# Three loads moved behind the first exchange of values and the transposes of a fused attention and feed-forward kernel

## The chip, the cores and the metric

The kernel runs on one core of a Trainium2 chip. The metric is the device time of one execution in microseconds (us). Three executions of the kernel before took 244.43, 244.81 and 245.82 us; their median is 244.81 us. The profile is of a further execution of its own.

## The reference, cut to what matters

The input x has 2048 rows of 512 bf16 numbers. It is normalised row by row, and the result feeds two branches. The output is x plus both.

```python
xn = _layernorm(x, axis=-1)
return x + _A_ref(xn, A_wq, A_wk, A_wv, A_wo, A_beta) + _B_ref(xn, B_w1, B_w2)

# A: 32 heads of 16 numbers, 4 segments of 512 rows, one after the other
logits = jnp.einsum('bhqd,bhkd->bhqk', qs, ks) * scale + mask    # causal, inside a segment
a_dot = jnp.einsum('bhqk,bhkd->bhqd', _softmax(logits, axis=-1), vs)
a_mem = num / den                        # phi(qs) against M and z of the segments before
o = g * a_mem + (1.0 - g) * a_dot        # g = sigmoid(beta), one number a head
M = M + jnp.einsum('bhld,bhle->bhde', phi(ks), vs)
z = z + jnp.einsum('bhld->bhd', phi(ks))
# then  o @ wo

# B: a feed-forward layer with 1792 hidden columns
out = jnp.einsum('bsf,fd->bsd', _silu(jnp.einsum('bsd,df->bsf', x, w1)), w2)
```

## The kernel before, in words

The work goes by the four segments of 512 rows (`NSEG`), and inside a segment by four slices of 128 columns (`DT`), each of which holds 8 heads. A slice of a segment is called u (u = 4 s + dt).

Per segment the rows are normalised (`ln`, lines 542 to 608): VectorE takes statistics of a block of 128 rows (BN_STATS, BN_AGGR), GpSimd makes the inverse deviation, VectorE writes the normalised block xn, and xn is transposed into xnT. For the first segment TensorE transposes; for the others SP issues a DMA transpose (line 602). xn lies in a ring of three buffers, so the fourth xn of a segment can't be written before the first transpose of it has landed. From xnT come k and q by slice (`k_tile`, `q_tile`), the values V (`v_tile`) and the hidden tiles h (`h_tile`: four matmuls into a PSUM bank, a tanh on ScalarE at line 1093, a multiply on VectorE at line 1097 which reads that bank for the last time).

The scores are worked in quads (`quad`, line 795): one quad fills four PSUM banks (psS), ScalarE takes the exponential of all of it (line 818), GpSimd cuts out what the causal mask forbids (line 834). There are 72 quads, nine for two slices. `pv` (line 848) multiplies the five quads of a slice by the values; it accumulates into two of four PSUM banks (ps), one for even and one for odd heads. Half of its matmuls read V, the other half VS, a copy of V with the upper and lower 64 partitions exchanged. `v_swap` (line 762) makes that copy with two DMAs of SP: the exchange of values. VectorE evicts the two banks to N and O (line 877).

phi(k) is made by ScalarE, GpSimd and VectorE in pkT, a ring of two, and transposed by DMA into phiK (line 709), from which the memory M is summed at the segment's end. den and norm work out the two divisors: VectorE and GpSimd make a small table, which goes out to DRAM and is read back in another shape (dD to Dg, dE to Dr, dZ to Zg, dR to R), all of it issued by SP; VectorE and GpSimd then multiply by it. `w2_rows` and `wo_rows` make the output rows of a segment during the next one.

What stands in which order on each engine isn't written out by hand. `Sched` (lines 98 to 261) plays the whole program through once with estimated durations while the kernel is built: each task has an engine, a duration, a time `vis` after which its result is taken to be there, a due time and the tasks it waits for; the ready task with the lowest due time goes next. The instructions are then emitted in that order, and each engine, SP among them, runs them strictly in order. `Dn(n)` is the due time of quad n: 12.5 + 2.3 n. A due time or a `vis` changes the order, not what is waited for on the chip.

All loads from DRAM stand at the beginning (lines 399 to 424). SP issues in this order: two blocks of x, half of wk, wv, half of w1, half of wk, the second 512 rows of x in two loads, the second half of w1, beta, wo, all of w2 (1792 KB), rows 1024 to 1535 of x (x8, the third block). ScalarE's queue issues two blocks of x and wq. The load of the last 512 rows (x12) waits for a free place in `x_all`, which holds three blocks. Only after these does SP come to the exchange of values and to the DMA transposes of the second segment.

Of the kernel before, what the change touches and what calls it, by code (L numbers as in the profile page):

```python
# [23 lines left out]
TPS = L // P  # L24
F = 1792
FT = F // P
# [238 lines left out]
def kernel(  # L265
# [38 lines left out]
    x_b = [Buf(x_r) for _ in range(NSEG)]  # L304
# [7 lines left out]
    w_o = sb([P, DT, D], BF16, "w_o")  # L312
# [58 lines left out]
    def Dn(n):  # L371
        return T0 + CYC * n
# [2 lines left out]

    xl = {}

    def load_x(t, n, eng, due, vis):
        def fn():
            e = nc.sync if eng == "SP" else nc.scalar  # L380
            c = x_b[t // TPS].idx * TPS + t % TPS
            e.dma_start(
                out=x_all[:, c : c + n, :],
                in_=x_flat[t * P : (t + n) * P, :].rearrange("(j p) d -> p j d", p=P),
            )
        k = A(eng, 0.5, fn, due=due, vis=vis, takes=(x_b[t // TPS],), label=f"x{t}")
        for i in range(n):
            xl[t + i] = k

    def load_w(dst, src, eng, due, vis):  # L390
        def fn():
            e = nc.sync if eng == "SP" else nc.scalar
            e.dma_start(out=dst, in_=src)
        return A(eng, 0.5, fn, due=due, vis=vis, label="w")

    def kv(w):
        return w.rearrange("(ko ki) n -> ki ko n", ki=P)
# [5 lines left out]
    def halves(dst, src, n, which):  # L403
        c = slice(0, n) if which == 0 else slice(n, None)
        return dst[:, :, c], kv(src)[:, :, c]

    C2, F2 = D // 2, F // 2
    ld_k = [load_w(*halves(w_k, A_wk, C2, 0), "SP", 0, 5.2)]
    ld_q = [load_w(*halves(w_q, A_wq, C2, 0), "ACTQ", 0, 5.4)]
    ld_v = load_w(w_v[:], kv(A_wv), "SP", 0, 7.5)  # L410
# [7 lines left out]
        bet[:], bass.AP(tensor=A_beta.tensor, offset=A_beta.offset, ap=[[0, P], [1, H]]),  # L418
        "SP", 0.35, 13.5,
    )  # L420
    ld_o = load_w(w_o[:], kv(A_wo), "SP", 0.4, 14.0)
    ld_2 = load_w(w_2[:], kv(B_w2), "SP", 0.5, 18.0)
    load_x(8, 4, "SP", 0.6, 19.0)
    load_x(12, 4, "SP", 0.7, 8.0)

    def pool(dur, fn, deps=(), due=0.0, **k):
        return A("POOL", dur, fn, deps, due, **k)

# [333 lines left out]
    def v_swap(s, due):  # L762
        ts = []
        for r in range(2):
            def f(r=r):
                a, b = slice(KB * r, KB * r + KB), slice(KB * (1 - r), KB * (1 - r) + KB)
                nc.sync.dma_start(out=VS_t[a, :, :], in_=V_t[V_b[s].idx][b, :, :])
            ts.append(A("SP", 0.6, f, v_ev[s], due, vis=6.0 if s == 0 else 4.2, takes=(VS_b[s],),
                        frees=(V_b[s], VS_b[s]), label="VS"))
        vs_ev[s] = ts  # L770

# [332 lines left out]
    def w2_rows(s, j, due):  # L1104
        t = s * TPS + j
        b = Buf(banks)
        ab = Buf(acc_r)

        def s2(ft):
            def f():  # L1110
                mm(b.tile[:], h_b[(s, ft)].tile[:, j * P : (j + 1) * P], w_2[:, ft, :],
                   ft == 0, ft == FT - 1)
            return (f, 0.216, (h_ev[(s, ft)],) + ((ld_2,) if ft == 0 else ()))

        g = group(b, [s2(ft) for ft in range(FT)], due, keep=1,
                  deps=[h_ev[(s, ft)] for ft in range(FT)], label=f"w2.{t}")
        for ft in range(FT):
            h_b[(s, ft)].n += 1
            g.frees.append(h_b[(s, ft)])

        def f_e():
            nc.vector.scalar_tensor_tensor(
                out=ab.tile[:], in0=b.tile[:], scalar=0.5, in1=xt(t), op0=ALU.mult,
                op1=ALU.add,
            )
        e = A("DVE", 0.6, f_e, [g], due + 4, takes=(ab,), frees=(b, ab, x_b[s]), label="acc")
        acc_ev[t] = (ab, e)

    def wo_rows(s, j, due):
        t = s * TPS + j  # L1130
        b = Buf(banks)
        ab, ae = acc_ev[t]

        def so(dt):
            def f():
                mm(b.tile[:], N_b[s].tile[:, dt, j * P : (j + 1) * P], w_o[:, dt, :],
                   dt == 0, dt == DT - 1)
            return (f, 0.216, (oT_ev[4 * s + dt],) + ((ld_o,) if dt == 0 else ()))

        g = group(b, [so(dt) for dt in range(DT)], due, keep=1,  # L1140
                  deps=[oT_ev[4 * s + dt] for dt in range(DT)], label=f"wo.{t}")
        N_b[s].n += 1
        g.frees.append(N_b[s])
        ob = Buf(o_r)

        def f_e():
            nc.vector.scalar_tensor_tensor(
                out=ob.tile[:], in0=b.tile[:], scalar=0.5, in1=ab.tile[:], op0=ALU.mult, op1=ALU.add
            )
        e = A("DVE", 0.6, f_e, [g, ae], due + 2, takes=(ob,), frees=(b, ab, ob), label="o_t")  # L1150

        def f_d():
            nc.sync.dma_start(out=out_flat[t * P : (t + 1) * P, :], in_=ob.tile[:])
        A("SP", 0.35, f_d, [e], due + 4, vis=1.75, frees=(ob,), label="out")

    def tail():
# [34 lines left out]
        for j in range(TPS):  # L1191
# [13 lines left out]
                nc.sync.dma_start(out=out_flat[t * P : (t + 1) * P, :], in_=ob.tile[:])  # L1205
            A("SP", 0.35, f_d, [e], 0, vis=1.75, frees=(ob,), label="out")

    ln(0, -4)
    for s in range(NSEG):
        b0 = 20 * s  # L1210
        if s + 1 < NSEG:
            ln(s + 1, Dn(1) if s == 0 else Dn(b0 - 4))
        if s == 0:
            for dt in range(DT):
                k_tile(0, dt, -2.9 if dt == 0 else Dn(5 * dt - 3 - dt % 2))
                q_tile(0, dt, -3 if dt == 0 else Dn(5 * dt - 2.9 - dt % 2))
# [67 lines left out]
```

## Time and profile before

| | us |
|---|---|
| Median of three executions | 244.81 |
| The profiled execution, its own time | 243.62 |
| Its span, first to last instruction | 241.9 |

So 1.7 us of the profiled execution lie around its span. In the span TensorE (PE) is busy 223.8 us, ScalarE (ACT) 178.5, VectorE (DVE) 170.2 and GpSimd (POOL) 164.0. The mean granted clock of TensorE is 0.979 of full speed.

The timeline has a row for each instruction or run of like instructions: its start, its length, engine, line, operation, output from input, count, and in brackets the idle time of its engine just before it with what ended that. SPq is SP's queue, where a row's length is the time that issuing took and not the time of the transfer; PEld is the loading of weights. The table of windows has, for each stretch, its length, the busy time and the count of instructions of PE, PEld, DVE, ACT and POOL, the granted clock, the mean busy share of the 16 DMA engines and the GB/s that they moved.

### The profile page before, as it was taken

The numbers are of one execution on the slowest core, as the hardware profiler recorded it, in microseconds if no ns is written. First come the engines' busy times: TensorE is split into PE (matmuls) and PEld (weight loads), VectorE is DVE, ScalarE is ACT, GpSimd is POOL, SyncE is SP. The second block draws the span as 40 slices with busy tenths as digits, with TensorE's granted clock in tenths as the row PEclk, the third lists the DMA queues.
The fourth block names the chain that finished last, engine by engine and source line by source line (L and its number), as shares of the span: only waits on it lengthen the run. The fifth ranks groups of instructions, "written<-read, shape, count | busy, mean of one in ns | idle before, by whom it ended". The sixth has DMA issues, their size and how long they took to land.

```text
span 241.9 us, 6809 instructions
## 1 busy us (share of the span) xinstructions
PE 223.8 (93%) x2812; PEld 104.8 (43%) x2812; DVE 170.2 (70%) x299; ACT 178.5 (74%) x160; POOL 164.0 (68%) x279
## 2 busy tenths in 40 slices
PE   7899579998999997999799999999998999999974
PEld 7644144433444433444344434454435433444431
DVE  4699497957977536799884599775656685576523
ACT  2599837997999793898797997788899888862000
POOL 7359838996997617799887789897755667454010
PEclk9999968999999997999999999999999999999999
DMA  6999940200354324311153320102352000143202
GB/s 191 354 357 335 143 63 3 45 2 3 65 103 100 91 79 125 101 45 30 39 119 73 85 54 3 43 8 98 101 121 72 27 4 11 25 121 107 69 25 87
DMA packets 31068, 21.33 MB, mean 88 GB/s; under 512 B 16116, under 2 KB 30140, under 8 KB 31036
## 3 DMA queue, kind: packets, MB, share of 16 engines
q1 hardware_dynamic: 29692, 20.10, 32.0%
q10 hardware_dynamic: 1344, 0.79, 1.1%
q8 instruction: 22, 0.36, 0.7%
q14 instruction: 10, 0.08, 0.1%
HBM read 11.87 MB, written 2.65 MB: 60 GB/s over the span
## 4 chain that ended last, share of the span: by engine, by line
PE 39%; POOL 16%; DMA 15%; DVE 12%; ACT 10%; SPq 4%; issue 3%; POOLq 0%; ACTq 0%; DVEq 0%
PE ps L500 32%; ACT Pt L818 8%; POOL Pt L834 8%; PE psS L500 6%; DMA xnT<-xn 3%; POOL kB L695 3%; DMA R<-dR 2%; DVE st L550 2%; SPq L1031 2%; DMA Dg<-dD 2%; POOL pq L999 2%; ACT hT L1093 2%; DMA dR<-Zr 2%; DVE hT L1097 2%; DMA Dr<-dE 1%
## 5 line engine op out<-in xcount | busy, mean ns | idle before, releaser
L818 ACT ACTIVATE Pt<-psS 128x2048 bf16<-128x2048 f32 x72 | 135.3, 1879 | 31.2 <-PE psS L500 26.5
L834 POOL TENSOR_SCALAR_AFFINE_SELECT Pt<-Pt 64x512 bf16<-64x512 bf16 (+1 forms) x144 | 95.2, 661 | 36.1 <-ACT Pt L818 30.9
L500 PE MATMUL ps<-xnT,w 128*128 128x512 bf16 x224 | 57.0, 383 | 0.1
L500 PE MATMUL ps<-w,hT 128*128 128x512 bf16 x196 | 48.7, 380 | 0.0
L1097 DVE SCALAR_TENSOR_TENSOR hT<-hT,ps 128x512 bf16<-128x512 bf16 x56 | 37.3, 679 | 10.6 <-ACT hT L1093 10.5
L1093 ACT ACTIVATE hT<-ps 128x512 bf16<-128x512 f32 x56 | 32.5, 599 | 4.9 <-PE ps L500 4.8
L500 PE MATMUL psS<-qT,kB 32*128 32x256 bf16 (+5 forms) x640 | 29.3, 267 | 2.6 <-ACT Pt L818 2.5
L500 PEld LDWEIGHTS <-w 128*128 128x128 bf16 x224 | 20.5, 99 | 25.7 <-issue 4.1
L500 PEld LDWEIGHTS <-hT 128*128 128x128 bf16 x224 | 20.3, 98 | 24.6 <-issue 3.1
L500 PE MATMUL ps<-Pt,VS 64*32 64x256 bf16 (+5 forms) x640 | 20.1, 273 | 4.7 <-DVE hT L1097 4.5
L500 PEld LDWEIGHTS <-kB 32*128 32x128 bf16 x640 | 12.4, 93 | 27.4 <-issue 25.1
L695 POOL TENSOR_SCALAR kB<-kT,pm 128x512 bf16<-128x512 bf16 x30 | 20.8, 702 | 4.2 <-DVE kT L690 2.7
L500 PE MATMUL ps<-Pt,V 64*32 64x256 bf16 (+5 forms) x640 | 21.8, 271 | 0.0
L500 PE MATMUL ps<-xnT,w_k 128*128 128x512 bf16 (+1 forms) x76 | 19.7, 366 | 0.5 <-DVE N L877 0.5
L877 DVE CAST N<-ps 128x512 bf16<-128x512 f32 x16 | 11.0, 687 | 12.0 <-PE ps L500 11.9
L500 PE MATMUL ps<-xnT,w_q 128*128 128x512 bf16 (+1 forms) x76 | 17.3, 346 | 2.2 <-DVE hT L1097 1.2
L999 POOL TENSOR_TENSOR pq<-pq,Dr 128x512 bf16<-128x512 bf16 x12 | 13.8, 1158 | 6.2 <-DMA Dr<-dE 5.9
L500 PEld LDWEIGHTS <-V 64*32 64x32 bf16 x640 | 14.1, 94 | 8.5 <-DVE hT L1097 2.5
L500 PE MATMUL ps<-w_o,N 128*128 128x512 bf16 x56 | 15.1, 384 | 1.2 <-DVE hT L1097 1.2
L500 PE MATMUL ps<-w_v,xnT 128*128 128x512 bf16 x64 | 16.0, 380 | 0.0
L500 PEld LDWEIGHTS <-VS 64*32 64x32 bf16 x640 | 13.0, 94 | 6.4 <-issue 3.8
L1063 DVE TENSOR_TENSOR N<-N,R 128x512 bf16<-128x512 bf16 x16 | 7.9, 500 | 9.6 <-DMA R<-dR 9.6
(82 smaller groups left out, 247.6 us busy)
## 6 DMA issues: line engine op xcount, KB each, us to landing
VS<-V SPq DMA_DIRECT2D x8, 264.0 KB
R<-dR SPq DMA_DIRECT2D x16, 128.0 KB
out_dram<-o_t SPq DMA_DIRECT2D x16, 128.0 KB
w<-in_B_w_dram SPq DMA_DIRECT2D x2, 896.0 KB
w<-in_B_w_dram SPq DMA_DIRECT2D x1, 1792.0 KB
Dr<-dE SPq DMA_DIRECT2D x12, 128.0 KB
x_all<-in_A_x_dram SPq DMA_DIRECT2D x2, 512.0 KB
N<-O SPq DMA_DIRECT2D x12, 64.0 KB
```

The lines of the kernel that those rows point to most:

```text
L500: nc.tensor.matmul(o, lhsT=l, rhs=r, start=start, stop=stop, **k)
L550: nc.vector.bn_stats(out=b.tile[:], in_=xt(t))
L695: nc.gpsimd.tensor_scalar(out=kB[u].tile[:, :, KB * r : KB * r + KB], in0=kT[u].tile[:].rearrange("p (a b) -> p a b", b=KB), scalar1=pm[:, ...
L818: nc.scalar.activation(out=pb.tile[:], in_=psS[:], func=AF.Exp, scale=SCALE)
L834: nc.gpsimd.affine_select(out=v, in_=v, compare_op=ALU.is_ge, fill=0.0, base=0, pattern=pat, channel_multiplier=-1,)
L877: nc.vector.tensor_copy(out=dst.tile[:, dt, :], in_=buf.tile[:])
L999: nc.gpsimd.tensor_tensor(out=pb.tile[:], in0=pb.tile[:], in1=rb.tile[:], op=ALU.mult)
L1031: nc.sync.dma_start(out=N_b[s].tile[r, ds, :], in_=O_b[s].tile[r, ds, :])
L1063: nc.vector.tensor_tensor(out=v, in0=v, in1=rb.tile[:], op=ALU.mult)
L1093: nc.scalar.activation(out=hb.tile[:], in_=b.tile[:], func=AF.Tanh, scale=0.5)
L1097: nc.vector.scalar_tensor_tensor(out=hb.tile[:], in0=hb.tile[:], scalar=1.0, in1=b.tile[:], op0=ALU.add, op1=ALU.mult)
```

## The change

Four loads leave the head of SP's list: wo, w2, x8 and x12. w2 is cut into two halves of 896 KB. A new function `late_loads`, called after the normalisation of the second segment has been entered, gives them due times and a time before which the planner doesn't place them. A row of `w2_rows` waits for the second half of w2 only from its eighth matmul on. The planner's `vis` of the first exchange of values goes from 6.0 to 4.2, that of all others. No arithmetic changes.

```diff
-    ld_o = load_w(w_o[:], kv(A_wo), "SP", 0.4, 14.0)
-    ld_2 = load_w(w_2[:], kv(B_w2), "SP", 0.5, 18.0)
-    load_x(8, 4, "SP", 0.6, 19.0)
-    load_x(12, 4, "SP", 0.7, 8.0)
...
-            ts.append(A("SP", 0.6, f, v_ev[s], due, vis=6.0 if s == 0 else 4.2, takes=(VS_b[s],),
+            ts.append(A("SP", 0.6, f, v_ev[s], due, vis=4.2, takes=(VS_b[s],),
...
-            return (f, 0.216, (h_ev[(s, ft)],) + ((ld_2,) if ft == 0 else ()))
+            return (f, 0.216, (h_ev[(s, ft)], ld_2[ft >= FT // 2]))
...
+    def late_loads():
+        def at(k, n):
+            k.ready = Dn(n)
+            return k
+
+        c = slice(0, FT // 2), slice(FT // 2, FT)
+        for i, n in ((0, 6), (1, 9)):
+            ld_2.append(at(load_w(w_2[:, c[i], :], kv(B_w2)[:, c[i], :], "SP", Dn(n), 5.5), n))
+        ld_o.append(at(load_w(w_o[:], kv(A_wo), "SP", Dn(12), 4.5), 12))
+        load_x(8, 4, "SP", Dn(14), 4.5)
+        load_x(12, 4, "SP", Dn(15), 8.0, [xl[8]])
+        at(xl[8], 14)
...
             ln(s + 1, Dn(1) if s == 0 else Dn(b0 - 4))
+            if s == 0:
+                late_loads()
```

The planner makes a new order of it on every engine. Three places matter. The first is SP's list after beta. Before, wo, w2 and x8 stand ahead of the exchange (VS) and of the transposes of the second segment (xnT1).

```order
L393 DMA bet_182<-in_A_beta_dram 128x32
L393 DMA w_o_74<-in_A_wo_dram 128x4x512
L393 DMA w_2_76<-in_B_w2_dram 128x14x512
L382 DMA x_all_70<-in_A_x_dram 128x4x512
L767 DMA VS_97<-V0_95 64x2112 x2
L602 DMA_TRANSPOSE xnT1_78<-xn1_80 128x4x128
L602 DMA_TRANSPOSE xnT1_78<-xn2_81 128x4x128
L602 DMA_TRANSPOSE xnT1_78<-xn0_79 128x4x128
L602 DMA_TRANSPOSE xnT1_78<-xn1_80 128x4x128
```

In the changed kernel the same place reads:

```order
L393 DMA bet_182<-in_A_beta_dram 128x32
L763 DMA VS_97<-V0_95 64x2112 x2
L598 DMA_TRANSPOSE xnT1_78<-xn1_80 128x4x128
L598 DMA_TRANSPOSE xnT1_78<-xn2_81 128x4x128
L598 DMA_TRANSPOSE xnT1_78<-xn0_79 128x4x128
L598 DMA_TRANSPOSE xnT1_78<-xn1_80 128x4x128
L393 DMA w_2_76<-in_B_w2_dram 128x7x512
L705 DMA_TRANSPOSE phiK0_100<-pkT0_98 128x4x128
L705 DMA_TRANSPOSE phiK0_100<-pkT1_99 128x4x128
L393 DMA w_2_76<-in_B_w2_dram 128x7x512
L393 DMA w_o_74<-in_A_wo_dram 128x4x512
L705 DMA_TRANSPOSE phiK0_100<-pkT0_98 128x4x128
```

The exchange and the four transposes now stand ahead of all late loads; the first half of w2 stands between the transposes of xn and those of phi(k), the rest follows after two of these. The load of x8 stands behind the last row shown, and the fourth transpose of phi(k) behind that.

The second place is on VectorE, from the last normalised block of the second segment (written into xn1) to the eviction of the first `pv` to N0. Before:

```order
L568 TENSOR_SCALAR xn1_80<-x_all_70,mv_153,rstd_154 128x512
L485 TENSOR_REDUCE gsum_184<-gm_183 128x3
L632 SCALAR_TENSOR_TENSOR pkT0_98,zc0_166<-kT0_82,pkT0_98 128x512
L550 BN_STATS st0_155<-x_all_70 128x6
L551 BN_AGGR mv_153<-st0_155 128x2
L1097 SCALAR_TENSOR_TENSOR hT3_117<-hT3_117,ps3_69 128x512
L632 SCALAR_TENSOR_TENSOR pkT1_99,zc0_166<-kT1_83,pkT1_99 128x512
L550 BN_STATS st1_156<-x_all_70 128x6
L551 BN_AGGR mv_153<-st1_156 128x2
L550 BN_STATS st2_157<-x_all_70 128x6
L551 BN_AGGR mv_153<-st2_157 128x2
L877 CAST N0_136<-ps0_66 128x512
```

In the changed kernel:

```order
L564 TENSOR_SCALAR xn1_80<-x_all_70,mv_153,rstd_154 128x512
L481 TENSOR_REDUCE gsum_184<-gm_183 128x3
L628 SCALAR_TENSOR_TENSOR pkT0_98,zc0_166<-kT0_82,pkT0_98 128x512
L1093 SCALAR_TENSOR_TENSOR hT3_117<-hT3_117,ps3_69 128x512
L628 SCALAR_TENSOR_TENSOR pkT1_99,zc0_166<-kT1_83,pkT1_99 128x512
L873 CAST N0_136<-ps0_66 128x512
```

The statistics of the third block (its x8 isn't there yet) have left this place; the four of them now stand some thirty rows further on, 14 instructions behind the third phi(k). hT3 is the last reader of bank ps3, which the first `pv` takes next. On TensorE nothing moves up to and with that first `pv` and the quad behind it.

The third place is on SP in the second segment, where the divisors are read back. Before:

```order
L963 DMA dD1_198<-den0_152 4x8x512
L709 DMA_TRANSPOSE phiK0_100<-pkT0_98 128x4x128
L1048 DMA dR0_192<-Zr0_176 128x128
L709 DMA_TRANSPOSE phiK0_100<-pkT1_99 128x4x128
L1055 DMA R0_139<-dR0_192 128x1x512
L1055 DMA R1_140<-dR0_192 128x1x512
L1055 DMA R2_141<-dR0_192 128x1x512
L969 DMA Dg1_179<-dD1_198 128x128
```

In the changed kernel:

```order
L959 DMA dD1_198<-den0_152 4x8x512
L1044 DMA dR0_192<-Zr0_176 128x128
L965 DMA Dg1_179<-dD1_198 128x128
L705 DMA_TRANSPOSE phiK0_100<-pkT0_98 128x4x128
L1051 DMA R0_139<-dR0_192 128x1x512
L1051 DMA R1_140<-dR0_192 128x1x512
L1051 DMA R2_141<-dR0_192 128x1x512
```

The read of Dg now stands ahead of the three reads of R and of both transposes. On VectorE the reciprocal of Dg moves ahead of the first multiply by R, where it stood behind it. Everything behind the first `pv` is ordered anew in this way, on all engines.

More of the change, by code (lines that the diff above doesn't have):

```diff
@@ L376, with load_x @@
     xl = {}
-    def load_x(t, n, eng, due, vis):
+    def load_x(t, n, eng, due, vis, after=()):
         def fn():
@@ L385, in fn, with load_w @@
             )
-        k = A(eng, 0.5, fn, due=due, vis=vis, takes=(x_b[t // TPS],), label=f"x{t}")
+        k = A(eng, 0.5, fn, due=due, vis=vis, seqdeps=after, takes=(x_b[t // TPS],), label=f"x{t}")
         for i in range(n):
             xl[t + i] = k
-    def load_w(dst, src, eng, due, vis):
+    def load_w(dst, src, eng, due, vis, after=()):
         def fn():
@@ L393, in fn @@
             e.dma_start(out=dst, in_=src)
-        return A(eng, 0.5, fn, due=due, vis=vis, label="w")
+        return A(eng, 0.5, fn, due=due, vis=vis, seqdeps=after, label="w")
     def kv(w):
@@ L407 @@
     C2, F2 = D // 2, F // 2
+    ld_o, ld_2 = [], []
     ld_k = [load_w(*halves(w_k, A_wk, C2, 0), "SP", 0, 5.2)]
@@ L1137, in f @@
                    dt == 0, dt == DT - 1)
-            return (f, 0.216, (oT_ev[4 * s + dt],) + ((ld_o,) if dt == 0 else ()))
+            return (f, 0.216, (oT_ev[4 * s + dt], ld_o[0]))
         g = group(b, [so(dt) for dt in range(DT)], due, keep=1,
```

## The prediction

> **What bounds the kernel now.** The page of the profile comes first: its span, TensorE's share, the granted clock and the traffic in 40 slices of 6.05 us each.
>
> ```profile
> span 241.9 us, 6809 instructions
> PE 223.8 (93%) x2812; PEld 104.8 (43%) x2812; DVE 170.2 (70%) x299; ACT 178.5 (74%) x160; POOL 164.0 (68%) x279
> PE   7899579998999997999799999999998999999974
> PEclk9999968999999997999999999999999999999999
> GB/s 191 354 357 335 143 63 3 45 2 3 65 103 100 91 79 125 101 45 30 39 119 73 85 54 3 43 8 98 101 121 72 27 4 11 25 121 107 69 25 87
> ```
>
> TensorE is the bound: 93% of the span. It falls off at two places before the tail, and at both the clock falls too: slices 5 and 6 (24 to 36 us) and the neighbourhood of slice 16 (91 to 97 us). The first lies where DMA traffic of 335 to 357 GB/s ends. So I read that place next, in the timeline of each engine, TensorE first.
>
> ```profile
> 27.06 0.40 PE L500 MATMUL ps<-Pt,V 64*32 64x512 bf16 x4
> 31.10 0.40 PE L500 MATMUL ps<-Pt,VS 64*32 64x512 bf16 x8 [3.64 <-DVE hT L1097]
> 27.90 0.09 PEld L500 LDWEIGHTS <-VS 64*32 64x32 bf16 x1 [0.74 <-DMA VS<-V]
> 33.52 1.88 ACT L818 ACTIVATE Pt<-psS 128x2048 bf16<-128x2048 f32 x1 [3.39 <-PE psS L500]
> ```
>
> The first `pv` begins at 27.06 and stands still for 3.64 us before its second bank. VS was late, but it was there at 27.90; what ends the wait is VectorE's hT, the last reader of that bank. ScalarE's exponentials wait 3.39 us in turn. Why hT came so late stands in VectorE's timeline and in the chain of waits, SP's issues beside them.
>
> ```profile
> 24.45 0.54 DVE L568 TENSOR_SCALAR xn<-x_all,mv,rstd 128x512 bf16<-128x512 bf16 x1
> 28.47 0.41 DVE L568 TENSOR_SCALAR xn<-x_all,mv,rstd 128x512 bf16<-128x512 bf16 x1 [3.48 <-DMA xnT<-xn]
> 30.39 0.66 DVE L1097 SCALAR_TENSOR_TENSOR hT<-hT,ps 128x512 bf16<-128x512 bf16 x1
> 20.13 8.25 DMA xnT<-xn
> 10.58 1.20 SPq L393 DMA_DIRECT2D w<-in_B_w_dram  x1
> 11.82 5.84 SPq L382 DMA_DIRECT2D x_all<-in_A_x_dram  x1
> 17.79 1.98 SPq L767 DMA_DIRECT2D VS<-V  x2
> ```
>
> VectorE needs the xn buffer that the first transpose reads. That transpose was issued at 20.13 and took 8.25 us to land, since wo, w2 and x8 were queued ahead. The same backlog blocked SP for 5.84 us in issuing x8. VectorE runs in order, so hT waited behind xn, and TensorE behind hT.
>
> **What the stall costs.** These are windows of the same trace.
>
> ```profile
> 18.00:24.00 6.00, 6.00 (x45) 2.52 (x44) 5.96 (x12) 5.80 (x6) 5.71 (x10) 1.00 1.12 340
> 31.10:39.00 7.90, 7.38 (x112) 3.54 (x112) 7.14 (x19) 4.50 (x4) 3.70 (x7) 0.57 0.17 36
> 31.50:32.00 0.50, 0.50 (x41) 0.50 (x28) 0.50 (x3) 0.00 (x0) 0.00 (x0) 0.53 1.15 250
> 38.00:38.50 0.50, 0.50 (x3) 0.18 (x2) 0.47 (x2) 0.50 (x1) 0.25 (x1) 0.65 0.00 0
> 24.00:60.00 36.00, 30.34 (x419) 13.56 (x418) 27.43 (x56) 27.84 (x28) 26.98 (x45) 0.91 0.31 44
> ```
>
> Behind the stall the clock is at half from about 31.5 to 38.2 us. From 31.10 to 39.00 TensorE was busy 7.38 us at a mean clock of 0.57, so 7.38 x 0.43 = 3.2 us of its work was lost beside the wait. The Trainium skill ("TensorE: Matmul & The Clock Gate", section on the HAM clock gate) says that an idle window of about 3.4 us halves the clock and a busy one of 3.4 us restores it; by one such window the loss would be an estimated 1.7 us and the sum 1.5 us smaller. The trace shows 6.7 us of half clock here, and I keep 3.2.
>
> **The change, part by part.**
>
> *The queue.* The loads kept ahead are eight blocks of x (1024 KB), wk, wq and wv (1536) and w1 (1792): 4352 KB, or 4.46 MB. Slices 1 and 2 of the page move 6.05 x (191 + 354) = 3.30 MB by 12.1 us; the other 1.16 MB at 357 GB/s are through by 15.3. The loads taken out are 2816 KB or 2.88 MB, 8.5 us at the 340 GB/s of the window of 18 to 24.
>
> ```profile
> 15.38 0.69 DVE L755 CAST V<-ps 128x512 bf16<-128x512 f32 x1
> 129.40 1.85 DMA Zg<-dZ
> 136.30 3.27 DMA R<-dR
> L709 SPq DMA_TRANSPOSE phiK<-pkT x12: 1190/1214/2017, 30.2 to 151.6; - x12
> 26.58 0.59 ACT L1093 ACTIVATE hT<-ps 128x512 bf16<-128x512 f32 x1
> 28.80 0.24 DVE L485 TENSOR_REDUCE gsum<-gm 128x3 f32<-128x96 f32 x1
> 28.96 0.68 DVE L632 SCALAR_TENSOR_TENSOR pkT<-kT,pkT 128x512 bf16<-128x512 bf16 x1
> 29.57 0.69 DVE L550 BATCH_NORM_STATS2 st<-x_all 128x6 f32<-128x512 bf16 x1
> 30.29 0.18 DVE L551 BATCH_NORM_AGGREGATE mv<-st 128x2 f32<-128x6 f32 x1
> ```
>
> V is complete at 16.07, so VS is issued into an empty queue. Two issues took 1.98 us; with 3.27 us to land, as a read of R in mid-kernel, VS is there by 21.3, nearly 6 us before it is wanted. The first xn is no earlier than before (its x is not among the moved loads), so its transpose is issued at 20.13 again. It takes 1.2 us to issue (the row of phiK: median 1214 ns). If its landing is like that of R, it is there by 24.6; the fourth xn wants the buffer at 24.99, the end of the third. VectorE's 3.48 us are gone, by a margin of 0.4.
>
> *The first `pv`.* hT needs the tanh, which ends at 27.17, as before: ScalarE ran ahead of the stall. VectorE gets there by 24.99 + 0.41 + 0.24 + 0.68 = 26.3 (xn, the sum for the gate, phi(k)), since the pair of statistics has gone. hT ends at 27.17 + 0.66 = 27.83, and TensorE goes on at 27.9 in place of 31.10: **3.2 us**. A wait of 0.45 us is left. I take the half clock to go with the long wait: **3.2 us** more.
>
> *The late loads.* SP ends its fourth transpose of xn near 27.4 (two issues of 1.2 from 24.99), issues half of w2, then the transposes of phi(k). Half of w2 is 0.92 MB, 2.7 us at 340 GB/s; the transpose behind it can land anywhere from 31 (nothing queued: 27.9 + 1.2 + 1.85, the landing of the small read of Zg) to 35 (the whole load, then 3.27). The reader of its buffer is ScalarE, whose next exp into pkT follows one quad:
>
> ```profile
> 28.95 1.08 ACT L1093 ACTIVATE hT<-ps 128x512 bf16<-128x512 f32 x2
> 35.29 0.62 ACT L623 ACTIVATE pkT<-kT 128x512 bf16<-128x512 bf16 x1
> 36.87 1.88 ACT L818 ACTIVATE Pt<-psS 128x2048 bf16<-128x2048 f32 x1 [0.96 <-POOL Pt L834]
> ```
>
> ScalarE ends its two tanh at 30.0, takes the quad (1.88) and the gate's tanh and wants pkT at about 32.1. The next exponential is queued behind that. So this costs 0 to 2.9 us; I take **-0.6**, since a quad of its own work lies in front. The second half of w2 and wo follow 2 us later; w2 is first read in the second segment, and nobody waits for it.
>
> *The statistics of the third block.* Four pairs of some 0.8 us (0.69 and 0.18, a little overlapped), three of which lay in the stall at no cost, now stand in a full stretch: 3.3 us of VectorE, 0 to 3.3 on the path. From 24 to 60 VectorE is busy 27.43 of 36 us; with 6.4 us less of span 2.2 us stay free. I take **-0.5**.
>
> *The second place.* SP's new order there touches a stall of the same build.
>
> ```profile
> 84.50 0.39 SPq L969 DMA_DIRECT2D Dg<-dD  x1
> 85.27 0.43 DVE L1063 TENSOR_TENSOR N<-N,R 128x512 bf16<-128x512 bf16 x1 [1.16 <-DMA R<-dR]
> 89.25 0.95 DVE L973 RECIPROCAL Dg<-Dg 128x128 f32<-128x128 f32 x1 [3.55 <-DMA Dg<-dD]
> 91.48 0.81 PE L500 MATMUL ps<-w_o,N 128*128 128x512 bf16 x3 [1.19 <-DVE hT L1097]
> 93.25 0.61 PE L500 MATMUL ps<-Pt,VS 64*32 64x512 bf16 x8 [0.63 <-DVE hT L1097]
> 90.00:98.00 8.00, 6.19 (x102) 2.86 (x100) 5.78 (x12) 4.06 (x3) 5.23 (x8) 0.79 0.40 120
> 82.45 1.94 SPq L1055 DMA_DIRECT2D R<-dR  x3
> ```
>
> Dg is issued at 84.50, behind a transpose (1.2) and three reads of R (1.94). VectorE waits for it 3.55 us, TensorE for VectorE 1.19 + 0.63 = 1.8 us, and the clock costs 6.19 x 0.21 = 1.3. With Dg ahead of these reads it comes some 3 us sooner. So up to 3.1 us are to be had; as the new order is new everywhere behind 30 us, the same may be lost elsewhere. Bounds 3.1 either way; I take **+1.0**, a third, because only this one place can be read from the order.
>
> Sum: 3.2 + 3.2 - 0.6 - 0.5 + 1.0 = **6.3 us**. From the profiled execution's 243.62 that is 237.3. The median of the runs is 1.19 us above that execution; from 244.81 it is **238.5 us**.
>
> **The rivals.**
>
> *Given back by engines that are full.* From 24 to 60 the four engines were busy 27 to 28 us each (TensorE 30.34 with 3.2 lost to the clock). In 29.6 us all would stand at 91 to 94%. In-order engines that full wait for each other. If a further 3 to 5 us of the 6.3 are given back, the time is 241.5 to 243.6. For it: ScalarE and VectorE were busy nearly as long as TensorE there. Against it: work can slip to 60 to 90 us, and TensorE at 93% of a span shows that it can be kept fed.
>
> *The change doesn't do what it says.* VS and xnT are late anyway, because the queue is still full or the transposes are slow, and hT waits as before: within 1.2 us of 244.8. For it: the margin of 0.4 us at xn, and a transpose in an empty queue isn't in the trace. Against it: the 8.5 us of transfers that stood in front are more than the 3.5 us of wait.
>
> *Slower: x8 comes too late.* x8 is now issued behind the third transpose of phi(k). VectorE reads it 14 instructions after writing that phi(k), at some 0.6 us each 8.4 us later; the transpose's issue, its own (a third of 1.94), 0.52 MB at 340 GB/s and the landing take 1.2 + 0.65 + 1.5 + 3.3 = 6.7. If it lands later, VectorE stands at the statistics, and queued behind them are the evictions of the third `pv`, so TensorE's banks stay full: the stall of before at another place, priced at its wait plus 3.2 us of clock. To lose more than the 6.3 + 1.2 us it has to wait over 4.3 us, which is to land over 6.0 us later than worked out here. Then the time is over 246. For it: x8 blocked SP for 5.84 us before, and w2's half and wo (1.4 MB, 4.2 us) go just ahead. Against it: they go out near 32 and should be through by 38, before x8 is issued. The Trainium skill ("DMA: Bandwidth & Descriptors", rules for kernel authors) says to issue a DMA early and wait late; by that rule the change has nothing to win. Here the early issue is what held the short transfers up.
>
> **How the numbers follow.** A measurement of this kernel can tell about 0.5%, 1.2 us, from no change. The forecast (faster by 3.3 us or more, likeliest 238.5) gets 0.66, gains given back to 241.5 to 243.6 gets 0.16, no effect 0.09, slower 0.09. So faster is 0.82, the same 0.09, slower 0.09. The best ends give 3.2 + 3.2 + 3.1 = 9.5 us or 235.3, with 0.4 us of spread between runs 234.9. Leaving out no effect and slower leaves out 0.18; the range is 234.9 to 243.4.
>
> **What would show it.** Right: no wait of VectorE for xnT near 25 us; the first matmul with VS by 28; a granted clock of 1.00 from 28 to 40; the eighth exponential near 30 in place of 33.52; at the second place, VectorE's wait for Dg under 2 us. Wrong: ScalarE idle before pkT near 32, VectorE idle before a BN_STATS near 50, or a new slice with half the clock behind a wait of over a microsecond.

## The result, and the profile after

The changed kernel takes 237.96 us (median of four executions, 236.88 to 238.85). The kernel before took 244.62 us beside it (243.88 to 245.82). The ratio is 0.9721, with a 95% interval of 0.966 to 0.9783: faster by 2.8%. The forecast was 238.5 us. Here and below the ratios leave out executions over 1.5% above the fastest of their kernel, the medians count all.

The profiled execution of the changed kernel took 238.85 us with a span of 237.1. First its page: span, busy shares, granted clock and traffic in 40 slices, here of 5.93 us each.

```profile
span 237.1 us, 6771 instructions
PE 218.1 (92%) x2780; PEld 105.0 (44%) x2812; DVE 171.1 (72%) x299; ACT 178.4 (75%) x160; POOL 163.2 (69%) x279
PEclk9999999999999999999999999999999999999999
GB/s 196 352 218 125 54 290 151 113 22 4 93 140 69 108 178 88 48 3 68 94 91 62 90 25 0 46 28 113 61 110 17 83 1 19 39 91 136 58 22 88
```

No slice of PEclk is below 9: both dips of the clock are gone. The traffic that stood in slices 3 to 5 has moved to slices 6 to 8 (30 to 47 us). Next the timeline where the stall was: TensorE, VectorE, ScalarE and SP's issues, in this order.

```profile
27.33 0.40 PE L496 MATMUL ps<-Pt,V 64*32 64x512 bf16 x4
28.21 0.40 PE L496 MATMUL ps<-Pt,VS 64*32 64x512 bf16 x8 [0.48 <-DVE hT L1093]
24.70 1.18 DVE L564 TENSOR_SCALAR xn<-x_all,mv,rstd 128x512 bf16<-128x512 bf16 x2
27.47 0.69 DVE L1093 SCALAR_TENSOR_TENSOR hT<-hT,ps 128x512 bf16<-128x512 bf16 x1 [0.46 <-ACT hT L1089]
30.18 1.90 ACT L814 ACTIVATE Pt<-psS 128x2048 bf16<-128x2048 f32 x1
34.20 0.63 ACT L619 ACTIVATE pkT<-kT 128x512 bf16<-128x512 bf16 x1 [2.04 <-DMA phiK<-pkT]
34.73 1.86 ACT L814 ACTIVATE Pt<-psS 128x2048 bf16<-128x2048 f32 x1
20.38 7.38 SPq L598 DMA_TRANSPOSE xnT<-xn  x4
27.81 0.58 SPq L393 DMA_DIRECT2D w<-in_B_w_dram  x1
28.48 2.52 SPq L705 DMA_TRANSPOSE phiK<-pkT  x2
31.06 0.57 SPq L393 DMA_DIRECT2D w<-in_B_w_dram  x1
```

The last two blocks of xn now run back to back (24.70, x2): VectorE no longer waits for xnT. hT waits only for its tanh, TensorE 0.48 us instead of 3.64, and the eighth exponential starts at 30.18 instead of 33.52. But a new wait stands behind it: ScalarE waits 2.04 us for a transpose of phi(k), issued at 28.48 behind half of w2. In the windows of this trace (length, busy time of PE, PEld, DVE, ACT, POOL, then the clock, DMA share and GB/s) it shows as idle TensorE.

```profile
28.00:40.00 12.00, 9.51 (x151) 4.66 (x159) 7.21 (x17) 9.78 (x11) 8.34 (x15) 1.00 0.81 228
34.00:38.00 4.00, 2.31 (x14) 0.92 (x13) 0.69 (x1) 3.71 (x4) 2.23 (x4) 1.00 1.10 340
```

From 34 to 38 us TensorE is busy only 2.31 of 4 us, while 340 GB/s of late loads arrive; its clock stays at 1.00.

The nth of the 72 exponentials is a clock that all versions share, since its order never changes. Its start in the two profiled executions, from ScalarE's rows:

| exponential | before | after | ahead by |
|---|---|---|---|
| 7 (the first behind the stall) | 33.52 | 30.18 | 3.34 |
| 8 | 36.87 | 34.73 | 2.14 |
| 10 | 43.57 | 39.62 | 3.95 |
| 14 | 54.09 | 50.76 | 3.33 |
| 15 | 58.33 | 53.27 | 5.06 |
| 27 | 89.81 | 85.10 | 4.71 |
| 28 (the second place) | 95.95 | 88.33 | 7.62 |
| 36 | 119.15 | 109.80 | 9.35 |
| 37 | 121.92 | 114.58 | 7.34 |
| 71 (the last) | 213.03 | 207.05 | 5.98 |
| end of span | 241.9 | 237.1 | 4.8 |

The number counts from 0. The gain comes up to 7, from 8 to 10, from 14 to 15, from 27 to 28 and up to 36; part of it goes again at 8, from 10 to 14, at 37 and behind. Two executions can't tell what of this is the change and what is chance: the medians differ by 6.66 us, these two by 4.77. That is what the experiments are for.

### The profile page after: what moved, and what is told of

It is laid out like the page before. It is cut to its first block, busy times and chain, and to the rows that moved or that the text cites. A ratio compares the mean times of both kernels' runs of the same rounds, so it can differ in the third digit from the quotient of the medians.

```text
span 237.1 us, 6771 instructions
## 1 busy us (share of the span) xinstructions
PE 218.1 (92%) x2780; PEld 105.0 (44%) x2812; DVE 171.1 (72%) x299; ACT 178.4 (75%) x160; POOL 163.2 (69%) x279
## 4 chain that ended last, share of the span: by engine, by line
PE 57%; POOL 12%; DMA 9%; ACT 9%; DVE 6%; issue 4%; SPq 2%; ACTq 0%; POOLq 0%; DVEq 0%
PE ps L496 47%; PE psS L496 10%; ACT Pt L814 7%; POOL Pt L830 6%; DMA phiK<-pkT 4%; DMA R<-dR 3%; POOL kB L691 2%; ACT hT L1089 2%; DMA dR<-Zr 2%; DVE hT L1093 1%; DVE pkT L628 1%; SPq L1051 1%; POOL pkT L622 1%; POOL pq L622 1%; DVE pq L628 1%
## 5 line engine op out<-in xcount | busy, mean ns | idle before, releaser
L830 POOL TENSOR_SCALAR_AFFINE_SELECT Pt<-Pt 64x512 bf16<-64x512 bf16 (+1 forms) x144 | 93.1, 647 | 40.5 <-ACT Pt L814 34.4
L496 PE MATMUL ps<-w,hT 128*128 128x512 bf16 x184 | 45.9, 380 | 1.2 <-issue 1.1
L496 PE MATMUL psS<-qT,kB 32*128 32x256 bf16 (+5 forms) x640 | 28.7, 261 | 4.9 <-ACT Pt L814 4.3
L496 PEld LDWEIGHTS <-w 128*128 128x128 bf16 x224 | 19.7, 97 | 24.8 <-issue 3.7
L691 POOL TENSOR_SCALAR kB<-kT,pm 128x512 bf16<-128x512 bf16 x30 | 22.2, 748 | 4.4 <-DVE kT L686 3.1
L496 PE MATMUL ps<-Pt,V 64*32 64x256 bf16 (+5 forms) x640 | 20.7, 260 | 0.0
L496 PE MATMUL ps<-Pt,VS 64*32 64x256 bf16 (+5 forms) x640 | 18.7, 261 | 1.2 <-DVE hT L1093 1.2
L496 PE MATMUL ps<-xnT,w_k 128*128 128x512 bf16 (+1 forms) x73 | 17.3, 344 | 0.9 <-DVE N L873 0.5
L496 PE MATMUL ps<-w_o,N 128*128 128x512 bf16 x54 | 14.1, 380 | 0.2 <-issue 0.2
L628 DVE SCALAR_TENSOR_TENSOR pkT<-kT,pkT 128x512 bf16<-128x512 bf16 x12 | 10.7, 889 | 4.7 <-POOL pkT L622 4.7
```

The costliest lines, as they stand in the source:

```text
L496: nc.tensor.matmul(o, lhsT=l, rhs=r, start=start, stop=stop, **k)
L628: nc.vector.scalar_tensor_tensor(out=dst_b.tile[:], in0=src_b.tile[:], scalar=0.0, in1=dst_b.tile[:], op0=ALU.max, op1=ALU.add, accum_out=acc,
L691: nc.gpsimd.tensor_scalar(out=kB[u].tile[:, :, KB * r : KB * r + KB], in0=kT[u].tile[:].rearrange("p (a b) -> p a b", b=KB), scalar1=pm[:, ...
L830: nc.gpsimd.affine_select(out=v, in_=v, compare_op=ALU.is_ge, fill=0.0, base=0, pattern=pat, channel_multiplier=-1,)
```

## The experiments

Most edits stand at the end, where the planner's list is emitted; `o` is that list. Each kernel comes with its comparison with the kernel before on the same chip, as a ratio with its 95% interval. Five kernels have idle work added, whose results nobody uses. The theory: the early loads hold up the short transfers behind them in SP's queue, so the queue is what pays, and the order is a side effect. The rivals: the new order pays; or the half clock does.

**The queue alone.** The order of before on all engines; only wo and w2 go out later, behind the second transpose of phi(k); x8 stays in front.

```diff
-    for t, k in sc.run():
+    o = [k for _, k in sc.run()]
+    late = [ld_o, ld_2]
+    o = [k for k in o if k not in late]
+    i = o.index(phi_k[0][1]) + 1
+    o[i:i] = late
+    for k in o:
```

> The kernel before with every engine's order as it was, but wo and w2 (whole) issued by SP behind the second transpose of phi(k); x8 stays in front. Theory (the queue was the cause; the wait of 3.6 us and the half clock behind it make 6.4 us): the first matmul with VS comes by 28.5, no half clock near 32 to 38, the wait at the second place (90 to 98 us) stays as it was, shifted; 6 to 6.5 us faster than before, ratio 0.973 to 0.976. Rival (the new order on the engines made the gain, the queue alone does nothing): within 1.2 us of before, ratio 0.995 to 1.005.

Measured: 239.37 us against 244.42, ratio 0.9778 (0.972 to 0.9836). Its timeline on TensorE, VectorE and SP:

```profile
28.64 0.40 PE L500 MATMUL ps<-Pt,VS 64*32 64x512 bf16 x8 [1.00 <-DVE hT L1097]
49.50 1.11 DVE L632 SCALAR_TENSOR_TENSOR pkT<-kT,pkT 128x512 bf16<-128x512 bf16 x1 [2.53 <-POOL pkT L626]
83.75 0.95 DVE L973 RECIPROCAL Dg<-Dg 128x128 f32<-128x128 f32 x1 [1.95 <-DMA Dg<-dD]
80.62 0.40 SPq L969 DMA_DIRECT2D Dg<-dD  x1
```

The first stall falls to 1.00 us without any change of order, and most of the gain is there, though 5.1 us by the medians is less than the 6 to 6.5 expected. The wait of 2.53 us for GpSimd at 49.50 is that of before (next part).

**The order alone.** The changed kernel, its late loads put back ahead of the exchange of values (x12 stays where it was).

```diff
+    early = [ld_o[0], ld_2[0], ld_2[1], xl[8]]
+    o = [k for k in o if k not in early]
+    i = o.index(ld_b) + 1
+    o[i:i] = early
```

> The changed kernel with every engine's order as changed, but wo, both halves of w2 and x8 issued right behind beta again, ahead of the exchange of values. Theory: the wait before the first matmul with VS is back at 3 to 4 us with half the clock behind it, ScalarE's wait for pkT is gone (2.0 us), the second place stays good; 3 to 5 us slower than the changed kernel, ratio to before 0.985 to 0.995. Rival (the order made the gain): as the changed kernel, ratio 0.970 to 0.976.

Measured: 241.69 us, ratio 0.9886 (0.9839 to 0.9933). On TensorE and VectorE:

```profile
32.06 0.61 PE L496 MATMUL ps<-Pt,VS 64*32 64x512 bf16 x8 [4.27 <-DVE hT L1093]
29.94 0.41 DVE L564 TENSOR_SCALAR xn<-x_all,mv,rstd 128x512 bf16<-128x512 bf16 x1 [4.64 <-DMA xnT<-xn]
```

The stall is back, longer than before's 3.64, and still 2.7 us are won by the medians. Part of it is at the stall itself: from the xn that waited to the first matmul with VS it takes 2.12 us here and 2.63 in before (28.47 to 31.10), where a pair of statistics stood ahead of hT. For the rest, these are the times between two exponentials in six executions of the old order (before and five experiments) and seven of the new (after and six experiments):

| from, to | old order | new order |
|---|---|---|
| 9, 10 | 3.29 | 2.45 or 2.46; 3.71 with w2 whole |
| 10, 14 | 10.51 to 11.08 | 11.03 to 11.15 |
| 14, 15 | 4.22 to 4.35 | 2.51 to 2.52 |
| 27, 28 | 6.14 in before, else 2.82 to 4.13 | 3.23 to 4.37 |
| 28, 36 | 23.20 to 24.64 | 21.37 to 21.47 |
| 36, 37 | 2.77 | 4.77 to 4.98 |
| 37, 46 | 23.89 to 24.77 | 24.65 to 26.25 |
| 14, 46 | 92.60 in before, else 89.06 to 91.15 | 89.19 to 90.84 |

The new order wins at some places and loses at others. At 10 it wins 0.8 us: in the old order two tanh, for pkT and pq, stand right ahead of this exponential, as ScalarE's rows of the kernel with the queue alone show:

```profile
38.04 0.63 ACT L623 ACTIVATE pkT<-kT 128x512 bf16<-128x512 bf16 x1
38.56 0.63 ACT L623 ACTIVATE pq<-qT 128x512 bf16<-128x512 bf16 x1
39.08 1.88 ACT L818 ACTIVATE Pt<-psS 128x2048 bf16<-128x2048 f32 x1
```

In the new order they come behind it, and some 0.5 us of this is given back by 14. At 15 it wins 1.7 us; this is the place in before's trace, VectorE first and TensorE behind it:

```profile
53.80 1.11 DVE L632 SCALAR_TENSOR_TENSOR pkT<-kT,pkT 128x512 bf16<-128x512 bf16 x1 [2.51 <-POOL pkT L626]
55.58 1.02 PE L500 MATMUL ps<-xnT,w_q 128*128 128x512 bf16 x4 [0.92 <-DVE V L755]
```

VectorE stood 2.51 us for GpSimd's part of phi(k), with V's eviction queued behind it, and TensorE for that. At 37 the new order loses 2.0, and after's trace has the same kind of wait on TensorE and VectorE:

```profile
111.81 1.02 PE L496 MATMUL ps<-xnT,w_q 128*128 128x512 bf16 x4 [1.75 <-DVE hT L1093]
110.04 1.11 DVE L628 SCALAR_TENSOR_TENSOR pkT<-kT,pkT 128x512 bf16<-128x512 bf16 x1 [1.25 <-POOL pkT L622]
```

From 14 to 46 the four old executions without before and without the next kernel have a mean of 90.7 us, the seven new ones 89.9: 0.8 us. With 0.5 at the stall and 0.3 net between 9 and 14, about 1.6 of the 2.7 us have a place in the traces. The interval of the ratio is 2.3 us wide; where the rest is, this table doesn't say.

**The second place alone.** The kernel before, with the read of Dg moved ahead of the reads of R on SP, and its reciprocal ahead of the first multiply by R.

```diff
+    o.remove(dg[1][0])
+    o.insert(o.index(dr[0]) + 1, dg[1][0])
+    o.remove(dg[1][1])
+    o.insert(o.index(nr[0]), dg[1][1])
```

> The kernel before with one thing moved: in the second segment SP reads Dg ahead of a transpose and the reads of R, and VectorE takes the reciprocal of Dg ahead of the first multiply by R. Theory: VectorE's wait of 3.55 us for Dg goes, TensorE's waits of 1.8 us near 91 to 93 and the half clock (1.3 us) go with it; 2 to 3 us faster, ratio 0.988 to 0.992, the first stall untouched. Rival (what is won there is given back to ScalarE and GpSimd within the segment): within 1 us, ratio 0.996 to 1.004.

Measured: 243.08 us, ratio 0.9947 (0.9902 to 0.9991). On TensorE, VectorE and SP:

```profile
34.32 0.61 PE L500 MATMUL ps<-Pt,VS 64*32 64x512 bf16 x8 [5.90 <-DVE hT L1101]
31.69 0.41 DVE L568 TENSOR_SCALAR xn<-x_all,mv,rstd 128x512 bf16<-128x512 bf16 x1 [5.41 <-DMA xnT<-xn]
86.67 0.94 DVE L974 RECIPROCAL Dg<-Dg 128x128 f32<-128x128 f32 x1
84.02 0.37 SPq L969 DMA_DIRECT2D Dg<-dD  x1
```

The wait for Dg is gone, as in after. The gain is 1.3 us by the medians, between the 2 to 3 expected and the rival's 1, and from exponential 14 to 46 it takes 89.06 us, 1.6 less than the mean of the four old executions. Before's 6.14 us from 27 to 28 was in part a bad draw: with Dg in its old place it takes 3.85 us in the kernel with the queue alone (a wait of 1.95 us for Dg, not 3.55). The same trace shows that the first stall varies too: 5.90 us here, in front of which nothing was changed, against 3.64.

**The changed kernel once more,** beside the next three on the same chip.

> The changed kernel as it is, as the measure for the other kernels of this group on the same chip. All theories: ratio to before 0.968 to 0.977.

Measured: 238.62 us (236.67 to 241.69, six executions) against 244.31, ratio 0.976 (0.9701 to 0.982). Its profiled execution took 236.67 us; exponentials 7, 8 and 71 start at 30.46, 34.92 and 206.42, so the new wait in front of 8 is there again. The mean clock of its executions is 0.993 to 1.00; a short dip may still come in some of them.

**Half of w2 behind the transposes of phi(k).** If the 2.04 us of ScalarE are due to that half, its place costs them.

```diff
+    o.remove(ld_2[0])
+    o.insert(o.index(phi_k[0][1]) + 1, ld_2[0])
```

> The changed kernel with the first half of w2 issued behind the second transpose of phi(k), so that no load stands between the transposes of xn and those of phi(k). Theory (the load in front of the transpose is what ScalarE waits for, 2.0 us before its exp into pkT, and TensorE's idle 1.6 us from 34 to 38 follows from it): that wait is under 0.3 us, the ninth exponential comes at 32.5 in place of 34.7, 1 to 2 us faster than the changed kernel. Rival (the wait is off the path, or comes back as a wait for the third transpose, which then has all of w2 and wo in front): within 0.7 us of the changed kernel.

Measured: 236.65 us (235.21 to 238.34), ratio 0.9701 (0.9646 to 0.9757). This is the fastest version: 2.0 us below the changed kernel in the same group by the medians, 1.4 by the ratios, whose intervals overlap. ScalarE's timeline and the window that was half empty:

```profile
32.20 0.65 ACT L619 ACTIVATE pkT<-kT 128x512 bf16<-128x512 bf16 x1
33.05 1.88 ACT L814 ACTIVATE Pt<-psS 128x2048 bf16<-128x2048 f32 x1 [0.20 <-POOL Pt L830]
```

```profile
34.00:38.00 4.00, 3.99 (x31) 1.52 (x29) 1.79 (x3) 3.78 (x4) 3.84 (x7) 1.00 1.09 366
```

The wait is gone, exponential 8 comes at 33.05, and TensorE is busy all of 34 to 38 us under the same traffic (366 GB/s). So it wasn't contention but the place in the queue. The last exponential comes at 205.10, 1.3 and 2.0 us sooner than in the changed kernel's two profiled executions.

**w2 whole.** The changed kernel with all of w2 in one load at the place of its first half.

```diff
-        for i, n in ((0, 6), (1, 9)):
-            ld_2.append(at(load_w(w_2[:, c[i], :], kv(B_w2)[:, c[i], :], "SP", Dn(n), 5.5), n))
+        for i, n in ((0, 6),):
+            ld_2.append(at(load_w(w_2[:], kv(B_w2), "SP", Dn(n), 5.5), n))
```

> The changed kernel with w2 whole (1792 KB) at the place of its first half; planned anew. Theory (the transpose of phi(k) lands behind the load, at 340 GB/s): ScalarE waits 2.7 us longer for pkT, 4.5 to 5 us in all, half the clock behind that; 3 to 5 us slower than the changed kernel, ratio to before 0.984 to 0.993. Rival (halves or whole don't matter, since the transfers are cut into the same packets): within 0.7 us of the changed kernel.

Measured: 244.03 us, ratio 0.9995 (0.9955 to 1.0035): nothing of the gain is left. The profiled execution took 245.47 us, 1.4 above the median, so the place of the wait is read from it, on ScalarE and TensorE, and its length only as that of one execution:

```profile
39.38 0.63 ACT L619 ACTIVATE pkT<-kT 128x512 bf16<-128x512 bf16 x1 [6.48 <-DMA phiK<-pkT]
41.83 0.61 PE L496 MATMUL psS<-qT,kB 32*128 32x512 bf16 x4 [6.21 <-ACT Pt L814]
```

ScalarE waits 6.48 us here, where 4.5 to 5 were expected, against 2.04 in the changed kernel. It starts 9.8 us after the issue of the first transpose (29.59), in the changed kernel 5.7 us. ScalarE's own work covers 3.3 and 3.7 us of the two, so that twice the bytes in front made three times the wait. The clock is at half here from 38.3 to 45.1 us. The halves are not a detail of the change: without them the stall is only moved.

**The stall put back, without the loads.** To price the stall, six statistics of a weight tile, which nobody reads, hold hT back on VectorE in the changed kernel. The next kernel also keeps TensorE at work during the wait with 16 matmuls whose result is overwritten.

```diff
+    t3 = h_ev[(0, 3)]
+    scr = sb([P, nc.vector.BN_STATS_DIM], F32, "scr")
+
+    def slow(old=t3.fn):
+        for _ in range(6):
+            nc.vector.bn_stats(out=scr[:], in_=w_v[:, 0, :])
+        old()
+    t3.fn = slow
```

> The changed kernel with six idle statistics on VectorE (6 x 0.6 = 3.5 us) right ahead of the hT that frees the second bank of the first product with the values; loads as changed. Theory (the wait and half the clock behind it are the price, however the wait comes about): the first matmul with VS near 31 in place of 28.2, clock 0.5 for 3 to 7 us behind it, 4.5 to 6.5 us slower than the changed kernel. Rival (only the wait counts, the clock is hidden): 2.5 to 3 us slower.

And in `pv`, ahead of its first matmul:

```diff
+            if u == 0:
+                for _ in range(16):
+                    mm(bufs[0].tile[:], ident[:], w_v[:, 0, :], True, True)
```

> The kernel e7 (the changed kernel with the stall put back by six idle statistics on VectorE) with 16 idle matmuls of 512 columns (3.5 us) on TensorE right ahead of the first product with the values, so that TensorE is busy through the stall. Theory: the first matmul with VS at the same time as in e7, clock 1.00 all through, 1.7 to 3.2 us faster than e7. Rival (the half clock is hidden behind ScalarE and VectorE): the same time as e7 within 0.7 us.

Measured: 241.01 us without the matmuls, ratio 0.9895 (0.9823 to 0.9966), and 241.71 us with them, ratio 0.9932 (0.9881 to 0.9984), in another group. The stall alone, on TensorE and ScalarE:

```profile
32.56 0.57 PE L496 MATMUL ps<-Pt,VS 64*32 64x512 bf16 x8 [4.20 <-DVE hT L1093]
35.30 1.88 ACT L814 ACTIVATE Pt<-psS 128x2048 bf16<-128x2048 f32 x1 [4.36 <-PE psS L496]
```

Its window behind the wait:

```profile
33.00:36.00 3.00, 2.75 (x89) 2.00 (x75) 1.48 (x5) 0.70 (x1) 0.00 (x0) 0.50 0.62 140
```

And with TensorE kept at work (one of the 16 added matmuls has no record):

```profile
28.66 3.63 PE L496 MATMUL ps<-w_v,ident 128*128 128x512 bf16 x15
33.57 0.40 PE L496 MATMUL ps<-Pt,VS 64*32 64x512 bf16 x8 [0.96 <-DVE hT L1096]
35.21 1.88 ACT L814 ACTIVATE Pt<-psS 128x2048 bf16<-128x2048 f32 x1 [3.58 <-PE psS L496]
```

Its window behind the wait:

```profile
33.00:36.00 3.00, 1.91 (x90) 1.51 (x91) 2.33 (x5) 0.79 (x1) 0.00 (x0) 1.00 0.91 261
```

The stall isn't quite the same: hT ends a microsecond later in the second kernel. The price of the clock is therefore read from the first matmul with VS on. From there to the next exponential it takes 35.30 - 32.56 = 2.74 us at half clock and 35.21 - 33.57 = 1.64 at full clock: 1.1 us. From exponential 7 to 10 it takes 8.02 and 7.95 us. So this dip, of 3.4 us, costs 1.2 us here, and the stall is the larger part. The ratios don't show the 1.2 us, but their intervals are 3.5 and 2.5 us wide.

Against the changed kernel of its group the stall alone is slower by 2.4 us in the medians and 3.3 in the ratios; the rival without a price for the clock gave 2.5 to 3, the theory 4.5 to 6.5. That alone doesn't settle it: the stall also hides the wait for the transpose of phi(k), since from exponential 7 to 10 it takes 8.02 us here and 9.44 in the changed kernel.

**The same in the order of before.** The kernel with the queue alone, first with five idle statistics ahead of hT, then with the 16 matmuls too.

```diff
+    t3 = h_ev[(0, 3)]
...
+        for _ in range(5):
+            nc.vector.bn_stats(out=scr[:], in_=w_v[:, 0, :])
```

> The kernel e1 (order of before, wo and w2 behind the second transpose of phi(k)) with five idle statistics on VectorE (3 us) right ahead of the hT that frees the second bank: the stall of before, without its cause. Theory now (e7 and e8 showed no loss by the half clock in the new order; in the order of before, quads 7 to 10 took 10.05 us at half clock and 8.75 in e1): first matmul with VS near 31.5, half clock for 3 to 7 us, quads 7 to 10 take 9 to 10 us, 3.5 to 4.5 us slower than e1. Rival (half clock costs its full 3.2 us in this order): 6 us slower than e1, as slow as before.

> The kernel e10 with 16 idle matmuls (3.5 us) on TensorE right ahead of the first product with the values, so that the stall stays and the clock is kept at 1.00. Theory now: the first matmul with VS as in e10, quads 7 to 10 take 8.5 to 8.8 us as in e1, 0.5 to 1.3 us faster than e10. Rival (half clock costs its full 3.2 us): 3 us faster than e10. Rival (half clock costs nothing at all): within 0.3 us by the quads.

Measured: 241.45 us, ratio 0.9846 (0.976 to 0.9932), and 241.93 us, ratio 0.9936 (0.9879 to 0.9993). The first of them, on TensorE:

```profile
32.52 0.62 PE L500 MATMUL ps<-Pt,VS 64*32 64x512 bf16 x8 [4.49 <-DVE hT L1097]
```

Its window behind the wait:

```profile
32.50:38.50 6.00, 5.75 (x106) 2.98 (x106) 5.76 (x16) 2.52 (x3) 2.08 (x4) 0.50 0.54 151
```

Here the half clock lasts 6 us, about as in before. From VS to exponential 7 it takes 2.79 us, against 1.69 in the kernel with the queue alone; from 7 to 10 it takes 9.18 against 8.75. That is 1.5 us for this dip, which lasts 6.8 us in all. Against the queue alone the whole stall costs 2.1 us by the medians, 1.7 by the ratios and 5.4 by the profiled executions, where 3.5 to 4.5 were expected. The second kernel is inconclusive for its question: the matmuls bridged the wait, but TensorE then waited for VectorE's eviction, and the clock fell all the same, as TensorE's row shows:

```profile
36.38 1.86 PE L500 MATMUL ps<-xnT,w_k 128*128 128x512 bf16 x4 [1.29 <-DVE N L880]
```

Its window behind the wait:

```profile
36.40:39.40 3.00, 3.00 (x18) 0.96 (x18) 2.83 (x9) 1.27 (x3) 2.06 (x4) 0.50 0.71 210
```

**The kernel before with TensorE kept at work.** The 16 matmuls alone, ahead of the first `pv` of the kernel before.

> The kernel before with 16 idle matmuls of 512 columns (16 x 0.216 = 3.5 us) put into TensorE's list right ahead of the first product with the values, into a bank that this product then overwrites: TensorE is busy while it would have waited, so the stall stays and only the clock is kept. Theory (half the clock costs 3.2 us beside the wait): clock 1.00 from 31 to 40, the first matmul with VS still near 31, 2.7 to 3.2 us faster than before, ratio 0.987 to 0.989. Rival by one window of 3.4 us at half clock: 1.7 us faster, ratio 0.993. Rival (the other engines are the bound there and the slow clock is hidden): no change, 0.998 to 1.002.

Measured: 245.54 us, ratio 1.0076 (1.0033 to 1.0119), slower by 0.8%; for its question it is inconclusive too. On TensorE and VectorE:

```profile
28.30 3.63 PE L500 MATMUL ps<-w_v,ident 128*128 128x512 bf16 x16
34.48 0.40 PE L500 MATMUL ps<-Pt,VS 64*32 64x512 bf16 x8 [2.23 <-DVE hT L1100]
37.29 2.29 PE L500 MATMUL ps<-xnT,w_k 128*128 128x512 bf16 x5 [1.29 <-DVE N L880]
31.86 0.41 DVE L568 TENSOR_SCALAR xn<-x_all,mv,rstd 128x512 bf16<-128x512 bf16 x1 [5.31 <-DMA xnT<-xn]
```

Its window behind the wait:

```profile
38.00:40.00 2.00, 2.00 (x16) 0.59 (x14) 1.83 (x7) 0.52 (x2) 1.76 (x3) 0.50 0.04 8
```

The wait for xnT was 5.31 us in this execution, longer than the matmuls last, and two waits of 2.23 and 1.29 us were enough to bring the clock to half.

## Why the prediction was right

The direction and the mechanism held, and the time is 0.5 us from the forecast. That it is so near is luck. Two terms of the sum had the wrong size, and both made the gain too large: the half clock was priced too high and the late loads too low. In the profiled executions the gain is accordingly 4.8 us, not the 6.3 that were worked out from one of them; the medians differ by 6.66.

**The first wait: 3.2 us on record.** Right. In the profiled pair the first matmul with VS goes from 31.10 to 28.21, 2.9 us, and exponential 7 gains 3.34. The queue alone brings it to 28.64; the other 0.4 us is the pair of statistics that no longer stands ahead of hT. The row that it rested on was a short draw: with the loads in front, TensorE waited 4.27 and 5.90 us in two other executions. That may be one reason why the medians differ by more than the profiled executions. The Trainium skill ("DMA: Bandwidth & Descriptors", rules for kernel authors) says to issue a DMA early and wait late; here that didn't pay for bulk loads in front of short transfers in one queue. The order alone, with the loads early, is at 241.69 us (ratio 0.9886), and the changed kernel at 237.96 (0.9721).

**The half clock: 3.2 us on record.** The mechanism was right, the size wrong. Not all of the work lost to the clock is time lost on the path. From the first matmul with VS to exponential 7 TensorE sets the pace, and half clock costs 1.1 us. Behind it TensorE has slack: in the old order the clock is at half for a further 3.4 us, which is up to 1.7 us of work, and from 7 to 10 it takes only 0.4 us more (9.18 against 8.75). So a dip of 3.4 us cost 1.2 us, and one of 6.8 cost 1.5. For before itself, 10.05 us from exponential 7 to 10 against 8.75 with the queue alone and 2.42 against 1.69 from VS to 7 give at most 2.0. So the term was 1.2 to 2.0 us too large.

The Trainium skill ("TensorE: Matmul & The Clock Gate", section on the HAM clock gate) puts one idle and one busy window of about 3.4 us; the estimate of 1.7 us made from it lies nearer to what was measured than my 3.2, though not for its reason: the dip did last two such windows, and the rest was hidden. Where it speaks of the idle window the traces differ: the clock fell behind waits of 2.23 and 1.29 us, and in before behind 1.19 and 0.63.

**The late loads: -0.6 us on record, 0 to -2.9 as bounds.** The step was right and the value too small. The transpose of phi(k) landed at 34.1, near the late end of the 31 to 35 given, and ScalarE, "idle before pkT near 32", which was listed as a sign against the forecast, waited 2.04 us. Moving that half of w2 wins 1.4 us by the ratios, and 1.3 and 2.0 by the last exponential. The cover was real, but too short: of the 5.6 us from 28.48 to 34.1 ScalarE's own work covered 3.6.

**The statistics of the third block: -0.5 us on record.** No wait appears before any of the four between 52.5 and 57.4 us. No run separates this term. But the old place would not have stayed free: with the queue alone, where two pairs still stand ahead of N's eviction, TensorE waits 1.30 us for it, in the fastest version 0.53.

**The second place: +1.0 us on record, 3.1 either way.** The value was right, for the reason given: Dg's place alone is worth 1.3 us by the medians and 1.6 between exponentials 14 and 46 of one execution, and the rest of the new order takes some of it back there, so that 0.8 is left. The profiled pair shows 2.5 us in that stretch (92.60 to 90.07), of which before's bad draw is the larger part.

**What the sum had not.** The gains of 0.8 us at exponential 10 and 1.7 at 15 and the loss of 2.0 at 37 were not read from the order, where only the place of the Dg wait had been looked at. They stand inside the 3.1 us either way. By the ratios the order alone is worth 1.1% and the queue alone 2.2%. Multiplied, 0.9778 x 0.9886 = 0.967, which is inside the interval of the version that has both without the misplaced half (0.9701); the changed kernel, at 0.9721 and 0.976, falls short of that by 1.2 to 2.2 us, about what the half costs.

**The rivals.** That the change does nothing falls with the first profile. That x8 comes too late did not happen: it is issued at 43 us and its first reader doesn't wait. That full engines give the gain back is not what took 1.2 us again at exponential 8: it was a transfer, since TensorE is busy there without a gap once the half of w2 is moved.

Added up by stretches, the profiled pair comes out. Up to exponential 7 it wins 3.3 us, the wait and the part of the half clock in front of it. From 7 to 14 it wins nothing (20.57 and 20.58 us). Against the queue alone, with 19.35, before loses 1.2 there, which is the rest of the half clock; the fastest version, with 18.87, wins a further 0.5 by the order; and the changed kernel loses 1.7 against that version by the half of w2. From 14 to 46 it wins 2.5, of which 1.9 is before's bad draw at the second place, and 0.1 from there to the last exponential. The tail takes 1.2 back: 4.8 us in all. The medians' 6.66 us ask for more than this pair shows. A longer first stall, as in the two other executions, would give it; that isn't shown.

What stays open: why the landing of the same transpose behind the same loads varies by 2 us between executions, what decides between a short and a long dip of the clock, and why the tail behind the last exponential was 1.2 us longer in the first profile of the changed kernel than in before.

## What to carry to other kernels

When a queue holds short transfers on which engines wait and bulk loads that nobody needs yet, put the bulk behind, and check the next short transfer behind each piece: 0.9 MB at the wrong place cost 1.3 to 2.0 us, 1.8 MB all of the gain. Work lost to a slow clock was more than the time lost here; price it by the engines that set the pace there. A wait for a DMA in one profiled execution is one draw: look for the same wait in other executions before it becomes a term.

## What the runs showed of the hardware

- Half clock came in two lengths. Eight traces have ten dips that begin and end inside the span: five of 3.4 us (3.41 or 3.42) and five of 6.8 us (6.82 or 6.83), added up from windows of 0.5 us. The wait doesn't tell which: 4.20 us brought a short dip, 4.49 us a long one, and so did 2.23 and 1.29 us shortly after each other.
- 16 matmuls of 512 columns, 3.63 us, bridge a wait of TensorE. The clock then stayed at 1.00 behind further waits of 0.96 and 0.47 us, and fell to half behind 1.04 and 1.29 us and behind 2.23 and 1.29 us.
- The transpose of xn behind 2.88 MB of loads makes VectorE wait 3.48, 4.64, 5.31 and 5.41 us in four executions.
